# Decay triangles and factors from chunk 1 on, with the gate work moved into the first units, in an mLSTM and mixture-of-experts kernel

## The chip, the cores and the metric

One core of one Trainium2 chip. The metric is the device time in microseconds of one execution; the kernel before took 758.47 us (median of 3 runs, 758.4 to 760.46).

## What is computed

Three layers follow one another on 4 batches of 768 tokens: an mLSTM with 8 heads of 40, a mixture of 8 experts with one expert for each token, and a gated layer of width 2048. Only the first and the beginning of the second are touched. Cut to that:

```python
for t in range(S):                      # S = 768, for each batch and head
    m_new  = maximum(f_gate[t] + m, i_gate[t])
    f_stab = exp(f_gate[t] + m - m_new)
    i_stab = exp(i_gate[t] - m_new)
    m = m_new
    C = f_stab * C + i_stab * outer(v[t], k[t])
    n = f_stab * n + i_stab * k[t]
    y[t] = sigmoid(o_gate[t]) * (C @ q[t]) / maximum(abs(n @ q[t]), 1)
x = y as 3072 tokens of 320
logits = normalised x @ normalised expert_emb.T / tau
expert = argmax(logits)                 # the experts and the last layer come behind it
```

## The kernel before

**Units.** The 768 steps are cut into 6 chunks of 128, and a unit is one chunk of one batch with all 8 heads: 24 units, chunk by chunk, so units 0 to 3 are chunk 0, 4 to 7 chunk 1, and so on. For a unit the kernel forms the scores (k against q, `scores_mm`, L483, 8 products), multiplies them by a 128 x 128 matrix of decays for each head (`scores_w`, L488), multiplies that with the values (`pv`, L546), adds what the state of the chunks before gives (`inter`, L533, `epilogue1`, `epilogue2`), divides and gates (`finish`, L581 and L584, on GpSimd), and brings the state forward (`state`, L497, the three products of weighted keys and values; `state_up`, L514 or L518; `state_decay`, L504).

**Decays, in two ways.** `scan(u)` makes the decay matrices from the row of forget factors of the unit, which `put_dec` stores to memory and `fload` loads back to all 128 partitions. In chunks below `CH`, here 0 and 1, one scan of VectorE runs over 8 x 128 columns (L431). From chunk `CH` on, the scan (L427) makes only the two triangles of 64 x 64 on the diagonal, 8 x 64 columns; the square beside them is a product of two factors, `far_mm` (L439) on TensorE, and ScalarE copies both out (L429, L444).

**Gates and factors.** The gates lie as 96 rows: the 32 pairs of batch and head three times, since the factors are kept as a rounded part and a rest. `gates_m` is the scan of the running maximum (L293), `gates_x` the two sums for the exponent of the forget factor (L298, L299), `gates_xi` that of the input gate, `gates_exp` the exponentials on ScalarE, `gates_z` takes the first column of each chunk out, `gates_e` scans the products of factors from a chunk's (and a half's) beginning (L334). `factors` casts and subtracts for the right factor `fb` (L371, L373), `suffix` makes the products up to a half's end in six steps (L360), for the left factor `fa`; `factor_a` casts that. `spread_b` writes `fb` into 8 masked copies, one for each head (L382, `rhsB`), `spread_a` writes `fa` into 4, one for each batch (L378, `lhsA`): ScalarE. `gates_pe` transposes input weights and decays into token order.

Chunks 0 and 1 have their gates made ahead of the loop; those of chunks 2 to 5 are made together, spread over iterations 0 to 6: the maximum in 0, the sums in 3, exponentials in 3 and 4, the scan of `gates_e` in 4, `gates_pe`, the first half of `suffix` and `spread_b` in 5, the rest in 6.

**Order.** The program is written out by hand (`manual_schedule`): every engine executes its instructions in the order of the text, so the place of a call in the loop over u is its place in each engine's queue. SP issues all the loads and stores, in one queue, with the eight stores that clear the expert slots (`zero_slots`, from iteration `Z0` = 1 on). Iteration u does the scores and the values of neighbouring units, then the routing of unit u-2: `route_t` (L590 to L592, three transpositions of the token rows `x` that GpSimd has finished, copied out by ScalarE, L594), `route_l` (L621 to L623, the logits, copied by VectorE, L625), and once in four units the choice of experts (`route_hot`), the ranks in the expert (`route_rank`, TensorE) and the slots (`route_slot`, VectorE), by which GpSimd scatters the rows.

## Time and profile before

| | us |
|---|---|
| median of 3 runs | 758.47 |
| the profiled execution | 757.6 |
| its span | 755.9 |
| prologue and unit 0, 0 to 17.6: TensorE, VectorE, ScalarE, GpSimd busy | 12.1, 12.0, 7.5, 8.9 |
| chunks 0 and 1, 17.6 to 66.3 | 36.1, 45.2, 23.6, 28.1 |
| chunks 1 to 5, 66.3 to 160.6 | 89.1, 83.3, 50.7, 61.3 |
| last units and first expert, 160.6 to 199 | 32.7, 27.5, 16.7, 22.3 |
| experts and last layer, 199 to 700 | 498.4, 335.4, 247.3, 109.6 |
| end, 700 to 756 | 46.4, 24.3, 21.5, 4.2 |

The engines are PE (TensorE, matmuls; PEld loads their weights), DVE (VectorE), ACT (ScalarE), POOL (GpSimd) and SP (the queue that issues the transfers). Busy time is to be read by stage: TensorE has 95% of the whole span, but in the second row of stages it isn't the busiest. In a timeline the bracket at a line's end gives the time that the engine stood idle ahead of the instruction and what released it.

### The profile page before, as it was taken

The page shows a single profiled execution, that of the slowest core. Times are in us where ns is not written, and L with a number is a line of the kernel's source. Part 1 is how long each engine was busy: PE and PEld are TensorE (multiplying, and loading weights), DVE is VectorE, ACT ScalarE, POOL GpSimd, SP SyncE. Part 2 cuts the span into 40 slices and gives each one's busy share as a digit, 9 for nine tenths or more (in the row PEclk, how much of TensorE's full clock was granted, in tenths as well). Part 3 has the DMA queues.
Part 4 walks back from the last instruction along what each step waited for, and adds up shares of the span by engine and source line. Part 5 has one row for each costly group of instructions (what it writes and reads, how often), then busy time and mean ns, then how long its engine had stood idle before and what let it go on. Part 6 is the DMA issues. An engine that isn't in the chain of part 4 may idle for free.

```text
span 755.9 us, 13328 instructions
## 1 busy us (share of the span) xinstructions
PE 714.8 (95%) x4724; PEld 671.3 (89%) x4724; DVE 527.7 (70%) x1095; ACT 367.3 (49%) x852; POOL 234.3 (31%) x348
## 2 busy tenths in 40 slices
PE   7696999988889999999999999999999999999994
PEld 6696898988889999999998889988889888899994
DVE  7998899896498989899986764545544554445542
ACT  4364455544466666667645443343343343334442
POOL 4562576794243433455401003003003003002011
PEclk9999999999999999999999999999999999999998
DMA  6985887662559767777732121201211201101000
GB/s 190 318 257 178 264 243 235 197 211 84 182 168 241 237 206 192 213 217 255 221 96 67 26 58 46 56 19 42 42 37 36 42 23 36 43 1 46 11 19 19
DMA packets 70490, 95.78 MB, mean 127 GB/s; under 512 B 31794, under 2 KB 56530, under 8 KB 70418
## 3 DMA queue, kind: packets, MB, share of 16 engines
q1 hardware_dynamic: 67346, 86.99, 39.6%
q0 software_dynamic: 3072, 7.89, 2.9%
q8 instruction: 38, 0.62, 0.3%
q14 instruction: 34, 0.28, 0.1%
HBM read 73.73 MB, written 17.19 MB: 120 GB/s over the span
## 4 chain that ended last, share of the span: by engine, by line
issue 41%; PE 24%; POOL 5%; DVE 1%; DMA 1%; POOLq 0%; ACT 0%; SPq 0%; ACTq 0%
PE acc L1230 12%; PE hp L138 11%; POOL out_dram L1275 3%; POOL xr L1381 2%; PE xt L1154 1%; DMA xr<-y 1%; POOL gap L1277 0%; DVE w L121 0%; POOLq L1725 0%; DVE xl L1172 0%; PE xt L1170 0%; DVE hs L1204 0%; DVE xl L1156 0%; DVE w L111 0%; ACT w L118 0%
## 5 line engine op out<-in xcount | busy, mean ns | idle before, releaser
L1230 PE MATMUL acc<-wout,hhl 128*128 128x320 f32 x1152 | 187.0, 309 | 0.0
L1230 PEld LDWEIGHTS acc<-wout,hhl 128*128 128x128 f32 x1152 | 175.9, 188 | 7.4
L1215 DVE TENSOR_TENSOR sg<-hp,sg 128x512 f32<-128x512 f32 (+1 forms) x112 | 68.8, 615 | 93.5 <-ACT sg L1214 87.1
L138 PE MATMUL hp<-xh,win 128*128 128x512 f32 (+1 forms) x560 | 131.0, 364 | 0.0
L1214 ACT ACTIVATE sg<-hp 128x512 f32<-128x512 f32 (+1 forms) x112 | 60.4, 539 | 124.6 <-PE hp L138 124.0
L1275 POOL DMA_INDIRECT out_dram<-o,tokd x24 | 24.0, 1002 | 312.1 <-ACT o L1259 308.5
L1217 DVE TENSOR_TENSOR hhl<-sg,hhl 128x512 fp32r<-128x512 f32 (+1 forms) x112 | 71.4, 637 | 70.3 <-ACT hhl L1216 69.8
L1230 PE MATMUL acc<-w,hs 128*128 128x320 f32 x636 | 104.7, 310 | 2.0 <-ACT hs L1203 1.0
L138 PEld LDWEIGHTS hp<-xh,win 128*128 128x128 f32 x560 | 93.9, 188 | 11.5 <-ACT xh L1420 0.2
L1216 ACT CAST hhl<-sg 128x512 fp32r<-128x512 f32 (+1 forms) x112 | 62.7, 559 | 80.1 <-DVE sg L1215 76.6
L1230 PEld LDWEIGHTS acc<-w,hs 128*128 128x128 f32 x636 | 96.8, 188 | 4.3 <-DVE hs L1204 1.7
L138 PE MATMUL hp<-xl,win 128*128 128x512 f32 (+1 forms) x336 | 85.7, 363 | 0.0
L110 POOL TENSOR_TENSOR w<-r,w 128x256 fp32r<-128x256 f32 x58 | 47.7, 823 | 105.4 <-ACT w L105 87.5
L138 PEld LDWEIGHTS hp<-xl,win 128*128 128x128 f32 x336 | 58.8, 189 | 10.9 <-DVE xl L1421 0.2
L138 PE MATMUL hp<-xh,w 128*128 128x440 f32 (+6 forms) x320 | 66.8, 338 | 0.0
L483 PE MATMUL sp<-qT,kblk 120*128 120x128 f32 x384 | 50.7, 289 | 2.6 <-DVE wm L488 2.6
L138 PEld LDWEIGHTS hp<-xh,w 128*128 128x128 f32 x320 | 51.4, 189 | 1.7
L483 PEld LDWEIGHTS sp<-qT,kblk 120*128 120x128 f32 x384 | 48.2, 204 | 3.4 <-DVE wm L488 2.8
L1203 ACT ACTIVATE hs<-hp 128x440 fp32r<-128x440 f32 (+6 forms) x64 | 30.2, 472 | 40.2 <-PE hp L138 38.0
L546 PE MATMUL op<-vp_in,wm 128*128 128x96 f32 (+1 forms) x368 | 45.3, 277 | 0.1
L546 PEld LDWEIGHTS op<-vp_in,wm 128*128 128x128 f32 x368 | 44.2, 196 | 0.3 <-DVE num L565 0.3
L138 PE MATMUL hp<-xl,w 128*128 128x440 f32 (+6 forms) x192 | 42.8, 331 | 0.0
(324 smaller groups left out, 1123.3 us busy)
## 6 DMA issues: line engine op xcount, KB each, us to landing
...
```

Of the source, the lines that this page charges most:

```text
L110: eng.tensor_tensor(out=t[:, 3 * P:5 * P].rearrange("p (c f) -> p c f", c=2), in0=r1[:, 0:2], in1=hif[:, 0:2], op=ALU.subtract)
L138: nc.tensor.matmul(hp, a, b, start=(i == 0), stop=(i == len(seq) - 1))
L483: nc.tensor.matmul(sp[:, h - hs.start], kblk[u % NLD][0:KR, h // 3, h % 3, :], qT[u][0:KR, h // 3, :], start=True, stop=True)
L546: nc.tensor.matmul(ops[:, h * NW:h * NW + n], wm[u][:, h], vp_in[u % NLD][:, h * DV:h * DV + n], start=True, stop=True)
L1203: nc.scalar.activation(out=hh, in_=hp, func=AF.Relu)
L1214: nc.scalar.activation(out=sg, in_=hp, func=AF.Sigmoid, scale=1.702)
L1215: nc.vector.tensor_tensor(out=g, in0=hp, in1=sg, op=ALU.mult)
L1216: nc.scalar.copy(hh, g)
L1217: nc.vector.tensor_tensor(out=hl, in0=g, in1=hh.bitcast(F32), op=ALU.subtract)
L1230: nc.tensor.matmul(acc_t[blk][i], hl if j == 2 else hh, w[:, DM:2 * DM] if j == 1 else w[:, 0:DM], start=(first and j == 0), stop=(last an ...
L1275: sc = nc.gpsimd.indirect_dma_start(out=out, out_offset=bass.IndirectOffsetOnAxis(ap=tokd[:, ti:ti + 1], axis=0), in_=o[:, i], in_offset=None)
L1381: eng.tensor_tensor(out=xr_t[blk], in0=xr_t[blk], in1=gated[:, t0:t0 + n].unsqueeze(2).to_broadcast([P, n, 3 * P]), op=ALU.mult)
```

## The change

`CH` becomes 1: wide scans of decays are left for units 0 to 3, and units 4 to 23 take triangles and factors. Chunk 0 has its gates made ahead of the loop on 32 rows only, from two loads instead of six; the other four loads (`load_gates(1)`, `load_gates(2)`) stand behind the loads of unit 2. The gates of chunks 1 to 5 are made together, 640 columns instead of 512, in iterations 0 to 3: in 0 `gates_m`, for the two late row groups too, and the masks; in 1 the sums and the exponential of the forget gates; in 2 `gates_z`, the store of the decay rows, the first half of `suffix`, `gates_e` and `spread_b`; in 3 the second half, `gates_pe`, `factor_a`, `spread_a` and the far product of unit 4. Two buffers are shared to make room (`est` is `fd`, `facA` lies in `mm`), and two copies of the masks go from VectorE to GpSimd. `gates_pe0` transposes chunk 0's input weights alone. In the loop `state(u)` stands ahead of `route_t`, `route_rank` behind `pv` and `route_slot` behind `epilogue2`; `scores_w` stands behind the next unit's scan from iteration 4 on; the zeros start in iteration 2.

In the rows below `L` is the line in each kernel's own text (lines of the changed kernel are two or three lower behind the prologue). ScalarE, from the copy of state products ahead of unit 5's rows to the first spread, in iterations 4 and 5 of the kernel before (`fb` the right factor, `rhsB` its spread, `pg` the transposed gates):

```order
L504 ACTIVATE Cst_188<-Cst_188,gdec 120x123 x3
L371 CAST fb<-est 96x256
L552 ACT_TABLE_LOAD
L552 ACTIVATE sg<-kvo 128x320
L395 COPY ei_tok<-pg 128x256
L396 COPY gdec<-pg 120x48
L464 COPY vp_in_122<-ei_tok 128x8
L594 COPY xT<-pr 128x384
L552 ACTIVATE sg<-kvo 128x320
L600 ACTIVATE sq,ss_all<-x 128x320
L504 ACTIVATE Cst_189<-Cst_189,gdec 120x123 x3
L382 ACTIVATE rhsB<-fb,hmask 96x4x64 x8
```

ScalarE in the changed kernel, iterations 2 and 3, from the cast of the right factor to the spreads of the left one:

```order
L364 CAST fb<-fd 96x320
L375 ACTIVATE rhsB<-fb,hmask 96x5x64 x8
L512 ACTIVATE Cst_185<-dC,mask_173 120x3x41 x3
L427 COPY pmb_135<-tri 64x8x64
L565 COPY num<-op 128x328
L393 COPY ei_tok<-pg 128x320
L394 COPY gdec<-pg 120x60
L462 COPY vp_in_119<-ei_tok 128x8
```

and behind these, in iteration 3:

```order
L592 COPY xT<-pr 128x384
L550 ACT_TABLE_LOAD
L550 ACTIVATE sg<-kvo 128x320
L405 COPY enT<-pe__517 128x2x8
L406 COPY enT<-pe__517 64x8
L598 ACTIVATE sq,ss_all<-x 128x320
L357 CAST fa<-mm 96x320
L371 ACTIVATE lhsA<-fa,bmask 96x320 x4
```

Both spreads stand within sixteen rows now, and between them the casts, the gates' copies and a table load. TensorE in iteration 3 of the changed kernel, where `r` is unit 1's logits, `tri` the far product of unit 4 and `sp` its scores; in the kernel before no far product stands ahead of unit 8:

```order
L402 MATMUL pe__517<-ident,emb 128x8
L403 MATMUL pe__517<-ident,emb 128x8
L404 MATMUL pe__517<-ident,emb 128x8
L619 MATMUL r<-enT,xT 128x128
L620 MATMUL r<-enT,xT 128x128
L621 MATMUL r<-enT,xT 128x128
L437 MATMUL tri<-rhsB,lhsA 64x512
L481 MATMUL sp<-qT,kblk_113 128x128 x8
```

The score product of unit 4 stands behind the far product. VectorE in iteration 2, from the denominators `dn` of unit 1, of the kernel before (`pmb` the decays of unit 3 and 4 by wide scans, `fg` the sums of the gates):

```order
L570 SCALAR_TENSOR_TENSOR dn<-num 128x8
L572 TENSOR_SCALAR dn<-dn 128x8
L574 RECIPROCAL dn<-dn 128x8
L431 SCALAR_TENSOR_TENSOR pmb_140<-fb,ident_h 128x1024
L488 TENSOR_TENSOR wm<-sp,pmb_141 128x1024
L570 SCALAR_TENSOR_TENSOR dn<-num 128x8
L572 TENSOR_SCALAR dn<-dn 128x8
L574 RECIPROCAL dn<-dn 128x8
L298 TENSOR_TENSOR fg<-fg,mm 96x512
L299 TENSOR_TENSOR fg<-fg,mm 96x512
L625 COPY logit_all<-r 128x8
L431 SCALAR_TENSOR_TENSOR pmb_141<-fb,ident_h 128x1024
```

VectorE in the changed kernel at the same place (`mm` holds the left factor, `fd` the scanned products, `tri` the triangles of unit 4):

```order
L568 SCALAR_TENSOR_TENSOR dn<-num 128x8
L570 TENSOR_SCALAR dn<-dn 128x8
L572 RECIPROCAL dn<-dn 128x8
L353 TENSOR_TENSOR mm<-mm 96x5x63
L353 TENSOR_TENSOR mm<-mm 96x5x62
L353 TENSOR_TENSOR mm<-mm 96x5x60
L328 SCALAR_TENSOR_TENSOR fd<-fg,fd 96x640
L366 TENSOR_TENSOR fb<-fd,fb 32x320
L367 TENSOR_TENSOR fd<-fd 96x5x64
L334 TENSOR_TENSOR gd<-pairm,fd 32x60
L486 TENSOR_TENSOR wm<-sp,pmb_136 128x1024
L425 SCALAR_TENSOR_TENSOR tri<-fb,id_128 128x512
```

Suffix products, the scan of 640 columns and the work on the factors stand between unit 1's denominators and unit 3's weighting of scores; the scan behind it is the narrow one. TensorE in iteration 7, an ordinary one (`op` the products with values, `pr` the transpositions, `dC` the state products, `ip` the state's part), before:

```order
L546 MATMUL op<-vp_in_124,wm 128x96 x7
L546 MATMUL op<-vp_in_124,wm 128x64
L590 MATMUL pr<-ident,x 128x128
L591 MATMUL pr<-ident,x 128x128
L592 MATMUL pr<-ident,x 128x128
L497 MATMUL dC<-vp_in_122,kw 120x123 x2
L497 MATMUL dC<-vp_in_122,kw 80x82
L533 MATMUL ip<-Cst_189,qT 128x3x41 x2
L533 MATMUL ip<-Cst_189,qT 128x2x41
L439 MATMUL tri<-rhsB,lhsA 64x512
```

and in the changed kernel:

```order
L544 MATMUL op<-vp_in_120,wm 128x96 x7
L544 MATMUL op<-vp_in_120,wm 128x64
L495 MATMUL dC<-vp_in_118,kw 120x123 x2
L495 MATMUL dC<-vp_in_118,kw 80x82
L588 MATMUL pr<-ident,x 128x128
L589 MATMUL pr<-ident,x 128x128
L590 MATMUL pr<-ident,x 128x128
L531 MATMUL ip<-Cst_184,qT 128x3x41 x2
L531 MATMUL ip<-Cst_184,qT 128x2x41
L437 MATMUL tri<-rhsB,lhsA 64x512
```

The state products have moved ahead of the transpositions.

The diff, cut:

```diff
-        R3, HP, CH = 3 * BH, P // 2, 2
+        R3, HP, CH = 3 * BH, P // 2, 1
         ig = ap1.tile([R3, S], F32, name="ig")
         fg = ap1.tile([R3, S], F32, name="fg")
-        for t, g in ((fg, f_gate), (ig, i_gate)):
-            for a in range(3):
+
+        def load_gates(a):
+            for t, g in ((fg, f_gate), (ig, i_gate)):
                 nc.sync.dma_start(out=t[a * BH:(a + 1) * BH], in_=g.rearrange("b h s -> (b h) s"))
+
+        load_gates(0)
...
-        est = ap1.tile([R3, NCH, P], F32, name="est")
+        est = fd
+        facA = mm[:, 0:(NCH - CH) * HP].rearrange("k (c t) -> k c t", t=HP)
...
-        def gates_m(c0, c1):
-            lo, hi = c0 * P, c1 * P
-            nc.vector.tensor_tensor_scan(out=mm[:, 1 + lo:1 + hi], data0=fg[:, lo:hi], data1=ig[:, lo:hi],
-                                         initial=(-1e30 if c0 == 0 else mm[:, lo:lo + 1]), op0=ALU.add, op1=ALU.max)
+        def rows_of(c0, c1, r=None):
+            r = r or slice(0, R3 if c0 else BH)
+            return (lambda t, o=0: t[r, c0 * P + o:c1 * P + o])
+
+        def gates_m(c0, c1, r=None):
+            v = rows_of(c0, c1, r)
+            nc.vector.tensor_tensor_scan(out=v(mm, 1), data0=v(fg), data1=v(ig),
+                                         initial=(-1e30 if c0 == 0 else mm[:, c0 * P:c0 * P + 1]), op0=ALU.add, op1=ALU.max)
 
         def gates_x(c0, c1):
-            lo, hi = c0 * P, c1 * P
-            nc.vector.tensor_tensor(out=fg[:, lo:hi], in0=fg[:, lo:hi], in1=mm[:, lo:hi], op=ALU.add)
-            nc.vector.tensor_tensor(out=fg[:, lo:hi], in0=fg[:, lo:hi], in1=mm[:, 1 + lo:1 + hi], op=ALU.subtract)
-            if c0 < 2:
-                gates_xi(c0, c1)
+            v = rows_of(c0, c1)
+            nc.vector.tensor_tensor(out=v(fg), in0=v(fg), in1=v(mm), op=ALU.add)
+            nc.vector.tensor_tensor(out=v(fg), in0=v(fg), in1=v(mm, 1), op=ALU.subtract)
 
         def gates_xi(c0, c1):
-            lo, hi = c0 * P, c1 * P
-            (nc.gpsimd if c0 else nc.vector).tensor_tensor(out=ig[:, lo:hi], in0=ig[:, lo:hi], in1=mm[:, 1 + lo:1 + hi], op=ALU.subtract)
-
-        def gates_exp_f(c0, c1):
-            lo, hi = c0 * P, c1 * P
-            nc.scalar.activation(out=fg[:, lo:hi], in_=fg[:, lo:hi], func=AF.Exp)
-
-        def gates_exp_i(c0, c1):
-            lo, hi = c0 * P, c1 * P
-            nc.scalar.activation(out=ig[:, lo:hi], in_=ig[:, lo:hi], func=AF.Exp)
-
-        def gates_exp(c0, c1):
-            gates_exp_f(c0, c1)
-            gates_exp_i(c0, c1)
+            v = rows_of(c0, c1)
+            (nc.gpsimd if c0 else nc.vector).tensor_tensor(out=v(ig), in0=v(ig), in1=v(mm, 1), op=ALU.subtract)
+
+        def gates_exp(t, c0, c1):
+            v = rows_of(c0, c1)
+            nc.scalar.activation(out=v(t), in_=v(t), func=AF.Exp)
...
-            if c0 >= CH:
+            if c0:
                 at = lambda t: t.rearrange("k c (a t) -> k c a t", t=HP)[:, c0:c1, :, 0:1]
                 nc.vector.tensor_copy(at(fd), at(fz))
                 nc.vector.memset(at(fz), 0.0)
-                return
-            if c0:
-                nc.vector.tensor_copy(fd[:, c0:c1, 0:1], fz[:, c0:c1, 0:1])
-            nc.vector.memset(fz[:, c0:c1, 0:1], 0.0)
-            if c0 == 0:
+            else:
+                nc.vector.memset(fz[0:BH, c0:c1, 0:1], 0.0)
...
-                factors()
-            gd = wk.tile([BH, n, B * G], F32, tag="gd", name="gd")
+            factors()
+            gd = wk.tile([BH, n, B * G], F32, tag="gd", name="gd", bufs=1)
...
-                nc.vector.tensor_copy(id2[a * HP:(a + 1) * HP],
+                nc.gpsimd.tensor_copy(id2[a * HP:(a + 1) * HP],
...
-        NZ, Z0 = E, 1
+        NZ, Z0 = E, 2
...
             load_v(0)
             gates_m(0, 1)
             gates_x(0, 1)
-            gates_exp(0, 1)
+            gates_xi(0, 1)
+            gates_exp(fg, 0, 1)
+            gates_exp(ig, 0, 1)
             gates_z(0, 1)
-            gates_m(1, 2)
-            gates_x(1, 2)
-            gates_exp(1, 2)
-            gates_z(1, 2)
             nc.sync.dma_start(out=emb, in_=expert_emb)
             norm_en1()
             load_k(1)
...
             load_k(2)
             load_q(2)
             load_v(2)
+            for a in range(1, 3):
+                load_gates(a)
             nc.sync.dma_start(out=tau_sb, in_=tau.unsqueeze(0).to_broadcast([E, 1]))
             keep_warm(ps_1.tile([P, 512], F32, tag="r", name="r"), 6)
-            gates_e(0, 2)
             scan0(0)
             scan0(1)
             kweigh(0)
             scores_mm(0)
-            gates_pe(0, 2)
+            gates_pe0()
             scores_w(0)
             vprime(0, nc.vector)
             scores_mm(1)
...
             for u in range(0, NU - 1):
                 if ok(u - 4):
                     finish(u - 2, nc.gpsimd)
+                if u == 2:
+                    gates_z(1, NCH)
+                    put_dec(1)
                 if ok(u + 2):
                     fload(u + 2)
                 if u == 3:
...
                     state(0)
                     scores_w(1)
                     state_up(0)
-                if u in (2, 5):
+                if u in (2, 3):
                     scores_w(u)
                 if u and ok(u + 1):
                     scan(u + 1)
-                if batch:
-                    route_rank(batch)
-                if u not in (0, 1, 2, 5):
+                if u > 3:
                     scores_w(u)
-                if batch:
-                    route_slot(batch)
-                    pend.extend(batch)
                 if u == 2:
                     norm_en2()
-                if u == 4:
-                    gates_z(2, NCH)
                 if 0 <= u - 1 - W0 < WH:
                     split_half_lo(u - 1 - W0)
                 if u == 0:
                     scan(1)
-                    gates_m(2, NCH)
+                    for a in range(1, 3):
+                        gates_m(0, 1, slice(a * BH, (a + 1) * BH))
+                    gates_m(1, NCH)
+                    masks()
                 if ok(u - 1):
                     pv(u - 1)
+                    if batch:
+                        route_rank(batch)
                     epilogue2(u - 1)
-                if u == 5:
-                    gates_pe(2, NCH)
-                if u in (5, 6):
-                    suffix(u == 6)
-                if u == 1:
-                    masks()
+                if batch:
+                    route_slot(batch)
+                    pend.extend(batch)
+                if u in (2, 3):
+                    suffix(u == 3)
+                if u == 3:
+                    gates_pe(1, NCH)
                 if ok(u + 1):
                     vprime(u + 1)
                     if units[u + 1][1] < CH:
                         kweigh(u + 1)
-                if u == 3:
-                    gates_x(2, NCH)
-                if u == 4:
-                    put_dec(1)
-                    gates_exp_i(2, NCH)
+                if u == 1:
+                    gates_x(1, NCH)
+                if u == 2:
+                    gates_exp(ig, 1, NCH)
+                if u:
+                    state(u)
                 rts = {2: [], 3: [0], 4: [1], 5: [2], 6: [3, 4]}.get(u, [u - 2] if ok(u - 2) else [])
                 if rts:
                     route_t(rts[0])
                 if u == NU - 2:
                     inter(u + 1, True)
-                if u > 4:
+                if u > 2:
                     sigm(u)
                 elif u < 2:
                     sigm(u + 1)
...
                     order_consts()
                 if u == 2:
                     finish(0, nc.gpsimd)
-                if u:
-                    state(u)
                 if u == 3:
                     prep_en()
                 if len(rts) > 1:
                     route_t(rts[1])
                     route_l(rts[0])
                 inter(u)
-                if ok(u + 1):
+                if ok(u + 1) and u != 3:
                     far_mm(u + 1)
                 for i in rts[-1:]:
                     route_l(i)
...
                     route_cnt(batch)
                 batch, newb = newb, None
                 state_decay(u)
+                if u == 1:
+                    gates_exp(fg, 1, NCH)
+                    gates_xi(1, NCH)
+                if u == 2:
+                    gates_e(1, NCH)
+                    spread_b(0, H)
                 if u == 3:
-                    sigm(u)
-                    gates_exp_f(2, NCH)
-                    gates_xi(2, NCH)
-                if u == 4:
-                    gates_e(2, NCH)
-                    sigm(u)
+                    factor_a()
+                    spread_a()
+                    far_mm(4)
                 for i in range(0 if u < US else 1 if u < NU - 5 else 2):
                     if pend:
                         scatter(pend.pop(0))
                 if ok(u + 1) and units[u + 1][1] >= CH:
                     far_out(u + 1)
                     kweigh(u + 1)
-                if u == 5:
-                    spread_b(0, H)
-                if u == 6:
-                    factor_a()
-                    spread_a()
                 if ok(u + 3):
                     load_k(u + 3)
                     load_q(u + 3)
```

## Rows read from the trace of the kernel before

**Rows 1.** Stage windows: stretch, its us, each engine's busy us, clock, DMA share, GB/s.

```profile
17.60:66.30 48.70, 36.08 (x283) 34.35 (x283) 45.22 (x70) 23.55 (x70) 28.09 (x39) 0.93 0.89 281
...
66.30:160.60 94.30, 89.11 (x778) 86.06 (x776) 83.33 (x211) 50.70 (x155) 61.31 (x76) 0.98 0.73 223
```

**Rows 2.** Timeline of TensorE: start us, duration, line, output<-inputs, idle time before and its releaser.

```profile
37.84 2.62 PE L483 MATMUL sp<-qT,kblk 120*128 120x128 f32 x16 [2.65 <-DVE wm L488]
...
66.31 3.48 PE L483 MATMUL sp<-qT,kblk 120*128 120x128 f32 x16
...
74.12 1.95 PE L483 MATMUL sp<-qT,kblk 120*128 120x128 f32 x16
```

**Rows 3.** Windows, columns as in rows 1: TensorE's pause and what follows it.

```profile
61.30:65.50 4.20, 0.00 (x0) 0.00 (x0) 3.95 (x9) 1.33 (x6) 2.56 (x4) 1.00 0.71 208
66.30:69.80 3.50, 3.50 (x25) 3.44 (x23) 3.09 (x12) 1.66 (x4) 0.00 (x0) 0.52 0.47 138
```

**Rows 4.** Timeline of the prologue, columns as in rows 2: SP's queue and VectorE.

```profile
2.19 1.35 SPq L158 DMA_DIRECT2D ig<-in_i_gate_dram  x3
...
12.40 0.34 SPq L282 DMA_DIRECT2D fb<-dec  x1
...
5.79 0.42 DVE L293 TENSOR_TENSOR_SCAN mm<-fg,ig 96x128 f32<-96x128 f32 x1 [1.29 <-DMA ig<-in_i_gate_dram]
...
9.96 0.15 DVE L327 COPY fd<-fg 96x1 f32<-96x1 f32 x1 [0.45 <-ACT fg L309]
...
17.55 2.29 DVE L431 TENSOR_TENSOR_SCAN pmb<-fb,ident_h 128x1024 f32<-128x1024 f32 x1 [1.47 <-DMA fb<-dec]
```

**Rows 5.** Timeline of VectorE; last, one group by form: busy us, mean ns.

```profile
25.17 1.31 DVE L350 COPY id<-ident 64x512 f32<-64x512 f32 x2
...
32.64 0.20 DVE L574 RECIPROCAL dn<-dn 128x8 f32<-128x8 f32 x1
...
39.14 0.64 DVE L298 TENSOR_TENSOR fg<-fg,mm 96x512 f32<-96x512 f32 x1
39.81 1.09 DVE L299 TENSOR_TENSOR fg<-fg,mm 96x512 f32<-96x512 f32 x1
...
45.88 1.21 DVE L334 TENSOR_TENSOR_SCAN est<-fg,fd 96x512 f32<-96x512 f32 x1
...
55.69 2.15 DVE L360 TENSOR_TENSOR facA<-facA 96x252 f32<-96x252 f32 x3
...
L360 DVE TENSOR_TENSOR facA<-facA 96x252 f32<-96x252 f32 x1 | 0.4, 364 | 0.0
```

**Rows 6.** Timeline of ScalarE; last, the state copies by form: busy us, mean ns.

```profile
47.54 1.28 ACT L552 ACT_TABLE_LOAD   x1
48.84 0.47 ACT L552 ACTIVATE sg<-kvo 128x320 f32<-128x320 f32 x1
...
52.97 3.29 ACT L382 ACTIVATE rhsB<-fb,hmask 96x256 fp32r<-96x256 f32 x8
...
L514 ACT ACTIVATE Cst<-dC,mask 120x123 f32<-120x123 f32 x12 | 3.5, 363 | 1.8 <-PE dC L497 1.7
```

**Rows 7.** An ordinary iteration: window, waits from 74 to 157 us, timeline.

```profile
128.00:134.60 6.60, 6.16 (x56) 5.99 (x55) 5.17 (x12) 3.63 (x12) 5.24 (x6) 1.00 0.62 186
...
DVE logit_all L625 <- PE r L623: 7.6, 10, 1.4
...
PE pr L590 <- POOL x L584: 4.2, 9, 0.8
...
136.10 1.71 POOL L581 TENSOR_TENSOR sg<-sg,dn 128x320 f32<-128x320 f32 x1
...
137.89 0.81 POOL L584 TENSOR_TENSOR x<-num,sg 128x320 f32<-128x320 f32 x1
...
138.75 0.33 PE L590 MATMUL pr<-ident,x 128*128 128x128 f32 x1 [0.44 <-POOL x L584]
...
139.14 0.73 PE L497 MATMUL dC<-vp_in,kw 128*120 128x123 f32 x6
```

6 lines of the change are left out of this document (4 added, 2 removed).

## The prediction

> **What bounds the kernel now.** I read the stage windows first. From 17.6 to 66.3 us VectorE is busy 45.2 of 48.7 us while TensorE has 36.1 [rows 1]: there the time is made by VectorE's queue, which holds the wide decay scans of units 2 to 7 and the gate work of chunks 2 to 5. From 66.3 to 160.6 us TensorE is busy 89.1 of 94.3 us, and a closed ring of all four engines sets the pace. The second view is the timeline at the score products, the first TensorE work of each unit: unit 4 starts at 37.84, waiting for VectorE; unit 7 at 66.31; unit 8 at 74.12 [rows 2]. The third is the clock: TensorE did nothing from 61.3 to 65.5, and afterwards ran at 0.52 of full speed, its 1.2 GHz level [rows 3], so that unit 7's product took 3.48 us where unit 8's took 1.95 [rows 2]. Everything behind unit 8 is untouched except for an order on TensorE, so the question has two parts: when does unit 8's score product start, and how long is one iteration behind it?
>
> **Prologue: a gain of 2.2 us at unit 1's scan.** Six gate loads stand first in SP's queue; three of them take 1.35 us to issue [rows 4], so the four that are moved back give 1.8 us to every load behind. The store of the decay row no longer waits for chunk 1's gates either, where VectorE waited 0.45 for an exponential [rows 4]; I count 0.4. Unit 1's scan waits for a broadcast issued at 12.40 and starts at 17.55 [rows 4], 5.15 us later. With the issue at 10.2 it starts at 15.3. The VectorE work that is taken out of the prologue (chunk 1's scans and sums) isn't counted again, because that load ends last either way.
>
> **Units 1 to 3 on VectorE: the point E, where the factor scan of all five chunks ends.** I carry the end of unit 1's denominator, 32.64 + 0.20 = 32.84 [rows 5], to the changed order, in which the same instructions stand in front of it and these come and go:
> - 2.25 off for the prologue, 1.3 off for the two mask copies that go to GpSimd [rows 5].
> - The two row groups of the gates loaded late: two scans of 0.42 us [rows 4], 0.84 at least. SP issues the last of these loads at about 15 us; at the 5.15 us of the broadcast in the same queue it lands at 20, where VectorE is through with unit 1's scan at 17.6. That makes up to 2.9; at the 2.2 us in which the first gate loads land (issued by 3.54, used at 5.79 [rows 4]), 0.84. I take 2.2, near the broadcast, since it is the same stretch of the same queue.
> - Five chunks where four stood: 0.3 for the longer maximum scan; the two sums 0.64 and 1.09 [rows 5] become 1.6 to 2.1, I take 1.9; 0.9 for the exponential that VectorE now waits for, with 0.4 of copies and zeroing.
>
> That is 32.84 - 2.25 - 1.3 + 2.2 + 0.3 + 1.9 + 0.9 + 0.4 = 35.0. Then come the first three suffix products, 2.15 us before [rows 5]; one of them took 0.36 where GpSimd left it alone [rows 5], so 1.3 to 2.6 with five chunks, I take 2.2. The factor scan, 1.21 us for 512 columns [rows 5], is 1.5 for 640. E = 38.7 us, between 36.0 and 39.7. Unit 4's scan is half as long, but it lies behind E, beside ScalarE's work.
>
> **From E to unit 4's score product: ScalarE takes over.** On TensorE the far product of unit 4 now stands directly ahead of unit 4's score product, and it needs both spread factors. Behind E on ScalarE, in order: the 8 right spreads, 3.29 us for 256 columns [rows 6], 3.6 for 320; a table load, 1.28 [rows 6]; 4 left spreads at the rate of the 8, 1.85; 18 small ones (three state copies, casts, other copies, a sigmoid, a square, and the two VectorE subtractions between them) and the far product, which I take at 0.34, a little under the 0.36 of a state copy [rows 6], 6.45. Sum 13.2. VectorE's second three suffix products fit beside it. Unit 4 starts at 38.7 + 13.2 = 51.9, between 49.2 and 52.9, where it started at 37.84.
> The table load shows 1.28 us and the sigmoid behind it starts at once, 48.84 after 47.54 [rows 6]. The Trainium skill (ScalarE: Activation LUTs, What ACT_TABLE_LOAD costs) puts a drain of about 1380 ns on top, 2.66 us for each switch of the set. By that the chain would be 1.4 us longer and the time 761.6; the trace doesn't agree, and the row decides.
>
> **Units 4 to 7.** All gate work is done by then, so TensorE sets the pace: 6.16 us busy in an ordinary iteration of 6.60 [rows 7], I take 6.2; iteration 6 has a second transposition, 0.4 us from 138.75 to 139.14 [rows 7], and a logit product that I put at twice that, 1.2 more. TensorE has stood still for some 4 us ahead of unit 4, as it did ahead of unit 7, so I charge the same loss of clock, 3.48 - 1.95 = 1.5. Unit 8 starts at 51.9 + 1.5 + 3 x 6.2 + 7.4 = 79.4, against 74.12: **a loss of 5.3 us**, between 1.1 (E at 36.0, and the clock stays up) and 6.3. Put shortly: four wide scans become narrow, worth 1 us each on VectorE, but the whole making of the factors now stands in front of unit 4, where three more units covered it.
>
> **State products ahead of transposes.** From unit 8 on TensorE waits at the transposes for the token rows of GpSimd in 9 iterations, 4.2 us in all, 0.8 at most [rows 7]. The three state products have their operands by then and take 0.73 us with the overlap [rows 7], some 0.6 of TensorE's time, so they fill all of these waits but what goes over 0.6: 3.9 us. They also used to stand between the transposes and the logit product, for which VectorE waits 7.6 us in 10 iterations [rows 7]. What decides is whether the rows then come earlier: in the ring shown, GpSimd's gating product is stretched to 1.71 us while VectorE's scan runs, and the transposes start at 138.75 after 0.44 of waiting [rows 7]. With logits 0.6 us earlier the scan starts and ends earlier, so the stretched product ends earlier too. I take a gain of 3.6; nothing is the lower end, 4.6 (TensorE's own pace in all iterations) the upper.
>
> **The rest, at nothing.** The rank products behind the probability products wait no longer for the one-hot rows, but units 20 to 22 are held by VectorE there. Slots made later delay the last four scatters by a microsecond or two, an estimate from the probability products that now stand ahead of them; the loads behind are waited for by nothing in the ring. Zeros a unit later: eight stores move by one unit each and leave unit 4's loads alone; the last lands about when the first scatter wants it.
>
> **Sum.** +5.3 - 3.6 = +1.7 us on the profiled execution, 757.6 us with a span of 755.9: 759.3. The median of the runs, 758.47, is 0.9 above that execution; the forecast is 760.2.
>
> **Rivals.**
> *Slower: the ring keeps its length.* From one transposition to the next run ScalarE's copy, sigmoid, square and decay, the far copy, then GpSimd's three products, one of them stretched to 1.71 by VectorE's scan. If this ring is 6.6 us long by itself, TensorE only waits somewhere else and the reorder gives at most 0.5: 758.47 + 5.3 - 0.5 = 763.3, and 764.3 with E at its late end. For it: GpSimd goes from the stretched product to the next without a gap. Against it: the next took 0.81 [rows 7]; without the stretch the ring is 6.6 - 0.9 = 5.7, below TensorE's 6.2. It decides from a gain under 2.5 us. The Trainium skill (GPSIMD Engine Reference, Key points) says that GpSimd and VectorE contend when VectorE has two SBUF inputs; by that rule the stretch stays wherever the scan falls, which is this rival.
> *Faster: the gate work packs well.* The late gate rows land before VectorE comes to them, GpSimd leaves the sums and suffix products alone (E at 36.0), unit 4 starts at 49.2: a loss of 2.6, or 1.1 if the clock stays up. With the reorder at 4.6 this is 758.47 - 2.0 to - 3.5: 755.0 to 756.5. For it: one suffix product at 0.36. Against it: 2.15 - 0.36 leaves 0.9 for each of the other two.
> *It doesn't do what it says:* the narrow scans save nothing as units 4 to 7 are TensorE's, and the state products gain nothing because the rows follow: loss of 1.1 to 2.6 alone, 759.6 to 761.1.
>
> **How the numbers follow.** A measurement of this kernel can tell 0.3% from no change, 756.2 to 760.7. Forecast, 0.44, spread 758.5 to 762.5: 0.26 within, 0.18 slower. Ring keeps its length, 0.20: slower. Packs well, 0.24: 0.20 faster, 0.04 within. Doesn't do it, 0.06: 0.04 within, 0.02 slower. Left over, 0.06: 0.04 faster, 0.02 within. Sum: faster 0.24, within 0.36, slower 0.40. The range leaves a tenth on each side: from the packed case's 755.0 to the ring's late end, 764.3.
>
> **What would show it.** In the changed trace: unit 1's scan near 15.3; VectorE waiting up to 2.5 us for gate rows behind it; the 640-column factor scan ending near 38.7; ScalarE without a gap behind that; TensorE idle, then unit 4's score product near 52 at the lower clock; unit 8's near 79; no wait for the token rows at the transposes, and iterations of 6.2 to 6.3. It is wrong if unit 4 starts before 48 (packing), or if the iterations stay at 6.6 (ring).

## The result

| kernel | median us | ratio to before, 95% interval |
|---|---|---|
| before | 758.43 (758.33 to 760.46, 4 runs) | |
| changed | 769.89 (766.37 to 771.2, 4 runs) | 1.0137 [1.0098, 1.0176] |

The changed kernel is slower by 1.4%. Forecast were 760.2 us and a range up to 764.3; the time lies outside it. Its profiled execution took 770.71 us with a span of 769.0, 13.1 more than before.

First the places at which the prediction measured: the score products in the timeline of TensorE (start, duration), of unit 23 in the kernel before, then of units 4, 5, 8 and 23 in the changed one.

```profile
174.78 1.95 PE L483 MATMUL sp<-qT,kblk 120*128 120x128 f32 x16
...
56.09 3.62 PE L481 MATMUL sp<-qT,kblk 120*128 120x128 f32 x16
...
64.30 1.95 PE L481 MATMUL sp<-qT,kblk 120*128 120x128 f32 x16
...
85.69 1.95 PE L481 MATMUL sp<-qT,kblk 120*128 120x128 f32 x16
...
188.22 3.01 PE L481 MATMUL sp<-qT,kblk 120*128 120x128 f32 x16
```

Unit 4 starts at 56.09 where the prediction had 51.9 and the kernel before 37.84; unit 8 at 85.69 where it had 79.4, against 74.12 [rows 2]; unit 23 at 188.22, against 174.78 before. So 11.6 of the 13.1 us are lost ahead of unit 8, 1.9 more up to unit 23, and 0.3 come back at the end.

Next the windows of the changed kernel (columns as in rows 1): the stage in which VectorE set the time, TensorE's pauses ahead of unit 4, and unit 4's first products.

```profile
17.60:66.30 48.70, 29.05 (x180) 27.61 (x180) 30.58 (x53) 21.12 (x55) 13.67 (x28) 0.72 0.56 157
...
43.90:56.00 12.10, 6.10 (x30) 5.24 (x31) 6.15 (x12) 9.63 (x27) 0.72 (x1) 0.50 0.53 168
56.10:59.70 3.60, 3.60 (x19) 3.60 (x17) 0.13 (x1) 2.62 (x7) 2.02 (x3) 0.50 0.07 20
```

VectorE, busy 45.2 us of this stage before [rows 1], has 30.6 now. The work is less, as the change meant it, but what lies in it takes longer, because the engines wait for one another. TensorE has 6.1 of 12.1 us ahead of unit 4 and runs at 0.50 of full speed, 1.2 GHz, there and in unit 4's products.

Why the factors come late, in the timeline of VectorE (idle time ahead of an instruction and its releaser in the bracket): unit 1's scan, the maximum scans of the two late row groups, that of all chunks, the two sums, unit 1's denominators, the suffix products and the factor scan.

```profile
16.39 2.29 DVE L429 TENSOR_TENSOR_SCAN pmb<-fb,ident_h 128x1024 f32<-128x1024 f32 x1 [3.46 <-DMA fb<-dec]
21.36 0.41 DVE L300 TENSOR_TENSOR_SCAN mm<-fg,ig 32x128 f32<-32x128 f32 x1 [2.67 <-DMA ig<-in_i_gate_dram]
22.12 0.42 DVE L300 TENSOR_TENSOR_SCAN mm<-fg,ig 32x128 f32<-32x128 f32 x1 [0.34 <-DMA ig<-in_i_gate_dram]
22.57 1.55 DVE L300 TENSOR_TENSOR_SCAN mm<-fg,mm,ig 96x640 f32<-96x640 f32 x1
...
28.30 1.13 DVE L305 TENSOR_TENSOR fg<-fg,mm 96x640 f32<-96x640 f32 x1
29.47 1.82 DVE L306 TENSOR_TENSOR fg<-fg,mm 96x640 f32<-96x640 f32 x1
...
38.44 0.20 DVE L572 RECIPROCAL dn<-dn 128x8 f32<-128x8 f32 x1
38.56 2.34 DVE L353 TENSOR_TENSOR mm<-mm 96x315 f32<-96x315 f32 x3
40.82 1.48 DVE L328 TENSOR_TENSOR_SCAN fd<-fg,fd 96x640 f32<-96x640 f32 x1
```

The point E of the prediction, the end of the factor scan, is 40.82 + 1.48 = 42.3, not 38.7. VectorE waits 2.67 and 0.34 us for the late gate rows.

And from there to unit 4: on ScalarE the copy of transposed rows, the table load and the sigmoid, the cast of the left factor and the left spreads; on VectorE the logit copy, behind which the left factor's rest stands; on TensorE the far product.

```profile
50.05 0.48 ACT L592 COPY xT<-pr 128x384 f32<-128x384 f32 x1 [0.89 <-PE pr L590]
50.55 1.28 ACT L550 ACT_TABLE_LOAD   x1
51.84 0.47 ACT L550 ACTIVATE sg<-kvo 128x320 f32<-128x320 f32 x1
...
53.04 0.44 ACT L357 CAST fa<-mm 96x320 fp32r<-96x320 f32 x1
55.00 1.92 ACT L371 ACTIVATE lhsA<-fa,bmask 96x320 fp32r<-96x320 f32 x4 [1.52 <-DVE fa L359]
...
54.28 0.17 DVE L623 COPY logit_all<-r 128x8 f32<-128x8 f32 x1 [3.45 <-PE r L621]
...
55.61 0.69 PE L437 MATMUL tri<-rhsB,lhsA 96*64 96x512 f32 x1 [1.37 <-ACT lhsA L371]
```

From E to unit 4 it is 13.8 us, against 13.2 forecast.

### The profile page after: what moved, and what is told of

It is laid out like the page before. It is cut to its first block, busy times and chain, and to the rows that moved or that the text cites. A ratio compares the mean times of both kernels' runs of the same rounds, so it can differ in the third digit from the quotient of the medians.

```text
span 769.0 us, 13342 instructions
## 1 busy us (share of the span) xinstructions
PE 720.2 (94%) x4725; PEld 675.9 (88%) x4725; DVE 521.4 (68%) x1088; ACT 371.0 (48%) x857; POOL 232.0 (30%) x349
## 3 DMA queue, kind: packets, MB, share of 16 engines
q1 hardware_dynamic: 67442, 85.94, 39.1%
## 4 chain that ended last, share of the span: by engine, by line
issue 41%; PE 23%; POOL 5%; DVE 2%; DMA 1%; POOLq 0%; ACT 0%; SPq 0%; ACTq 0%
PE acc L1226 11%; PE hp L138 10%; POOL out_dram L1271 3%; POOL xr L1377 2%; PE xt L1150 1%; DMA xr<-y 1%; DVE w L121 0%; POOL gap L1273 0%; DVE hs L1200 0%; DVE xl L1152 0%; DVE w L111 0%; DVE fr L1295 0%; POOLq L1721 0%; DVE xl L1168 0%; PE xt L1166 0%
## 5 line engine op out<-in xcount | busy, mean ns | idle before, releaser
L138 PEld LDWEIGHTS hp<-xh,win 128*128 128x128 f32 x560 | 94.0, 188 | 11.4 <-ACT xh L1416 0.2
L481 PEld LDWEIGHTS sp<-qT,kblk 120*128 120x128 f32 x384 | 50.4, 211 | 1.5 <-DVE pmb L454 0.9
L544 PE MATMUL op<-vp_in,wm 128*128 128x96 f32 (+1 forms) x368 | 44.3, 274 | 1.4 <-DVE wm L486 1.4
```

Of the source, the lines that this page charges most:

```text
L138: nc.tensor.matmul(hp, a, b, start=(i == 0), stop=(i == len(seq) - 1))
L481: nc.tensor.matmul(sp[:, h - hs.start], kblk[u % NLD][0:KR, h // 3, h % 3, :], qT[u][0:KR, h // 3, :], start=True, stop=True)
L544: nc.tensor.matmul(ops[:, h * NW:h * NW + n], wm[u][:, h], vp_in[u % NLD][:, h * DV:h * DV + n], start=True, stop=True)
```

## Experiments: which part of the change costs what

In what follows an iteration is counted from the score product of its unit to that of the next. The theory after the two traces (A): triangles and early factors lose 11.6 us ahead of unit 8; state products ahead of the transpositions win 1.9 us in the eleven ordinary iterations behind it (8, 9, 11 to 13, 15 to 17, 19 to 21: 69.0 us against 70.9); and ranks behind the probability products, slots behind the denominators lose 3.7 us in the four with a choice of experts (10, 14, 18, 22: 33.5 against 29.8). The last was an edit that the prediction had put "at nothing". In the changed kernel, iteration 14, VectorE reads the ranks at 132.75 and TensorE waits to write logits into the same bank (both are the tile `r`):

```profile
132.75 0.14 DVE L687 TENSOR_TENSOR sl__1490<-r,oh_all 128x32 f32<-128x32 f32 x1
...
133.03 0.46 PE L619 MATMUL r<-enT,xT 128*128 128x128 f32 x2 [1.65 <-DVE sl__1490 L687]
```

Four kernels put these parts together one by one. `e1_state_alone` is the kernel before with

```diff
+                if u:
+                    state(u)
                 rts = {2: [], 3: [0], 4: [1], 5: [2], 6: [3, 4]}.get(u, [u - 2] if ok(u - 2) else [])
...
-                if u:
-                    state(u)
```

> The kernel before with one move: the state products ahead of the transpositions. Theory A (from the two traces: the eleven ordinary iterations behind unit 8 are shorter by 1.9 us in sum): 756.5 us, between 755.5 and 757.5, and the wait at the transpositions for the token rows, 4.2 us before, near 1. Rival (the ring keeps its length): 758.4, with the waits moved to another instruction.

`e2_order_alone` is that with ranks and slots moved too:

```diff
-                if batch:
-                    route_rank(batch)
...
-                if batch:
-                    route_slot(batch)
-                    pend.extend(batch)
...
                     pv(u - 1)
+                    if batch:
+                        route_rank(batch)
                     epilogue2(u - 1)
+                if batch:
+                    route_slot(batch)
+                    pend.extend(batch)
```

> The kernel before with the change's whole order of the ordinary loop: state products ahead, rank products behind the probability products, slots behind the denominators. Theory A (the slots are made later, and the logit product waits for the bank that they read; 3.7 us in the four iterations 10, 14, 18, 22): 756.5 + 3.7 = 760.2, between 758.8 and 761.2. Rival (those four iterations are longer for another reason, such as late loads): as the kernel with the state products alone, 756.5.

`e3_ranks_back` is the changed kernel with that second diff reversed, `e4_triangles_alone` with both reversed.

> The changed kernel with rank products and slots where they stood before. Theory A: 769.9 - 3.7 = 766.2, between 764.5 and 767.5, with no wait of the logit product for the slots. Rival (another reason): 769.9.

> The changed kernel with the order of the ordinary loop undone altogether (state products behind the transpositions, ranks and slots as before): triangles, factors and early gates alone. Theory A: the loss stands in front of unit 8, 11.6 us by the trace, so 766.2 + 1.9 = 768.1, between 766.5 and 770. Rival (part of the loss behind unit 8 belongs to the order): under 765.

| kernel | median us | ratio to before, 95% interval |
|---|---|---|
| e1, state products | 757.29 | 0.9987 [0.9971, 1.0003] |
| e2, with ranks and slots | 758.44 | 0.9996 [0.9980, 1.0012] |
| e3, changed, ranks and slots back | 768.47 | 1.0122 [1.0089, 1.0154] |
| e4, triangles and early gates alone | 768.36 | 1.0127 [1.0097, 1.0157] |

The median of before was 758.63 here. The triangles with the early gates make nearly all of the loss: 9.7 us in e4, somewhat less than theory A had. In the kernel before the state products win about 1 us and the ranks and slots lose about 1; in the changed one the state products win nothing that shows (768.47 with them, 768.36 without) and the ranks and slots lose 1.4. Each of these is within the intervals. For its other parts theory A doesn't hold as it stood: e2 and e3 lie outside their ranges, and e1, inside its own, has 70.8 us in the eleven ordinary iterations, where the kernel before has 70.9, and still waits 2.9 us at the transpositions.

Nor are the 11.6 us ahead of unit 8 all the triangles'. In e4 unit 8 starts at 82.87, 8.8 us behind the kernel before and 2.8 ahead of the changed one. Of these 2.8 us 1.0 is ahead of unit 4: in iteration 3 of the changed kernel the transpositions stand behind state products that themselves wait for ScalarE, so that ScalarE's copy of the transposed rows waits 0.89 us (at 50.05, above); in e4 it doesn't wait, and from E to unit 4 it is 12.8 us instead of 13.8. Another 0.6 is iteration 6 (7.84 us against 7.23), and 1.0 iteration 7, by the ranks (7.55 against 6.56, and 6.55 in e3). In e4, on ScalarE and TensorE:

```profile
48.98 0.47 ACT L592 COPY xT<-pr 128x384 f32<-128x384 f32 x1
...
82.87 1.95 PE L481 MATMUL sp<-qT,kblk 120*128 120x128 f32 x16
```

The traces show the ranks more plainly than the time: from unit 8 to unit 23 it takes 102.5 us in the changed kernel and 98.9 with ranks and slots back, 98.5 in e1 and 102.1 in e2, 3.6 us both times. In iterations 10, 14, 18 and 22 alone it is more, 33.5 against 27.0 and 27.6 against 32.1, but the ordinary iterations move the other way by 2.9 and 0.8. With ranks and slots back, slots are read at 131.13 and the logits follow without a wait:

```profile
131.13 0.17 DVE L687 TENSOR_TENSOR sl__1475<-r,oh_all 128x32 f32<-128x32 f32 x1
...
132.00 0.38 PE L619 MATMUL r<-enT,xT 128*128 128x128 f32 x2
```

The bank is only part of it. In iteration 22, which has 1.9 of the 3.7 us of theory A, TensorE doesn't wait for it. The kernel before stands twice there, 1.52 us ahead of the last rank products and the products with the values, and 0.57 ahead of the state's part (`ip`); with the ranks behind those products it stands once, for 2.08, and afterwards ran at 0.50 of full speed instead of 1.00. From the state's part to unit 23's scores it then takes 4.36 us instead of 2.31. Timelines and windows of the kernel before and of the changed one:

```profile
169.49 0.22 PE L671 MATMUL r<-oh_all,ones 128*128 128x24 bf16 x3 [1.52 <-DVE oh_all L651]
...
172.47 1.57 PE L533 MATMUL ip<-Cst,qT 120*128 120x123 f32 x12 [0.57 <-ACT xT L594]
...
172.47:174.70 2.23, 2.23 (x19) 2.19 (x20) 1.30 (x5) 1.17 (x4) 1.79 (x3) 1.00 0.20 78
...
183.86 2.86 PE L531 MATMUL ip<-Cst,qT 120*128 120x123 f32 x12 [2.08 <-ACT xT L592]
...
183.86:188.20 4.34, 4.34 (x19) 4.25 (x20) 1.50 (x7) 1.73 (x5) 2.10 (x4) 0.50 0.10 38
```

That the medians show 1.2 us (e1 to e2) or 1.4 (changed to e3) of the 3.6 has two reasons in sight. A profile is one execution: e1's was the shortest of its ten (754.89, up to 759.31), e2's the second longest (759.8, from 756.86); what the others lose, and where, isn't shown. And e3 gives 2.5 us back behind unit 23: from its scores to the first expert's accumulation it takes 23.9 us, the changed kernel 21.3, as VectorE's last weighting of scores stands for 2 us there and TensorE behind it. What releases it, the profile doesn't settle.

## Experiments: why the factors come late

Theory B: VectorE's queue up to the factor scan, then ScalarE's up to the left spreads, decide when unit 4 starts; each microsecond taken out of either comes off. Each kernel here adds one edit to the one before it. `e5_gates_sooner`, the changed kernel with

```diff
             fload(1)
+            for a in range(1, 3):
+                load_gates(a)
             load_k(2)
             load_q(2)
             load_v(2)
-            for a in range(1, 3):
-                load_gates(a)
```

> The changed kernel with the four late gate loads issued ahead of unit 2's loads instead of behind them. Theory B (the gate work on VectorE is late because it waits for these rows, 2.67 and 0.34 us behind unit 1's scan): the waits go, the 640-column factor scan ends near 39.3 instead of 42.3, unit 4's score product starts near 53.1 instead of 56.1, 766.9 us (765.5 to 768.5). Rival (another wait stands behind it, such as unit 2's loads, now later): unit 4 within 0.5 of 56.1, 769.9.

`e6_input_gate_sooner`:

```diff
+                if u == 1:
+                    gates_xi(1, NCH)
                 if ok(u + 1):
                     vprime(u + 1)
...
                 if u == 1:
                     gates_exp(fg, 1, NCH)
-                    gates_xi(1, NCH)
```

> As the kernel with the gate loads sooner, and GpSimd's subtraction for the input gates issued ahead of the values of unit 2, so that it no longer runs beside VectorE's two sums. Theory B (the sums took 1.13 and 1.82 us because GpSimd worked beside them; 0.8 and 1.36 is what 640 columns cost at the rate of before): factor scan and unit 4 earlier by another 0.8 us, 766.1. Rival (it stretches the scan or the product that it now stands beside as much): no change.

`e7_sigmoid_later`:

```diff
-                if u > 2:
+                if u > 3:
                     sigm(u)
...
                     far_out(u + 1)
                     kweigh(u + 1)
+                if u == 3:
+                    sigm(u)
```

> As the kernel before it in this list, and unit 3's sigmoid with its table load moved behind the spreads. Theory B (ScalarE's queue leads from the factor scan to unit 4): unit 4's score product earlier by another 1.7 us, near 50.6, 764.4. Rival (VectorE or TensorE leads there): under 0.4 us.

`e8_kept_warm`, with `wt_` in the bank of `ip`:

```diff
+                if u == 3:
+                    keep_warm(wt_, 10)
                 if u:
                     state(u)
...
                     prep_en()
+                    keep_warm(wt_, 10)
...
+                    keep_warm(wt_, 8)
                     far_mm(4)
```

> As the kernel before it in this list, and 28 idle products on TensorE (identity by identity, into a bank that nobody reads) in the three pauses ahead of unit 4's score product. Theory B (the pauses cost the clock): unit 4's score product 1.95 us instead of 3.6 and the logit products ahead of it 0.7 shorter, 762.3. Rival (the clock falls all the same, or the idle products stand in the way): 764.4 or more.

| kernel | median us (before 758.58 beside e5 to e8) | factor scan ends | unit 4 starts | unit 8 starts |
|---|---|---|---|---|
| changed | 769.89 | 42.3 | 56.09 | 85.69 |
| e5, gate rows sooner | 767.26 | 40.9 | 54.65 | 83.52 |
| e6, input gates sooner | 767.40 | 38.9 | 52.70 | 81.46 |
| e7, sigmoid later | 764.36 | 39.1 | 51.18 | 80.85 |
| e8, idle products | 766.43 | 41.2 | 55.03 | 83.04 |

VectorE's timeline in e5 (unit 1's scan and the late scans) and e6 (unit 1's scan and the second sum):

```profile
17.45 2.29 DVE L429 TENSOR_TENSOR_SCAN pmb<-fb,ident_h 128x1024 f32<-128x1024 f32 x1 [4.53 <-DMA fb<-dec]
...
19.77 1.23 DVE L300 TENSOR_TENSOR_SCAN mm<-fg,ig 32x128 f32<-32x128 f32 x2
21.04 1.55 DVE L300 TENSOR_TENSOR_SCAN mm<-fg,mm,ig 96x640 f32<-96x640 f32 x1
...
16.13 2.29 DVE L429 TENSOR_TENSOR_SCAN pmb<-fb,ident_h 128x1024 f32<-128x1024 f32 x1 [3.65 <-DMA fb<-dec]
...
27.07 0.82 DVE L306 TENSOR_TENSOR fg<-fg,mm 96x640 f32<-96x640 f32 x1
```

In e5 the late scans start behind unit 1's scan without a wait, so the 3.0 us are gone; but in this execution that scan itself starts at 17.45 instead of 16.39, held by its own load, and about half is given back: 1.4 us at unit 4, 2.6 in the median. The edit isn't shown to be the reason: e6 and e7 have the same loads in the same order and start it at 16.13 and 16.36, e8 at 17.49. In e6 the second sum falls from 1.82 to 0.82 us once GpSimd doesn't work beside it. The first stays at 1.13. Unit 4 comes 1.95 us sooner than in e5, 1.0 by the sum and the rest by that load, and yet the median doesn't fall: in the profiles loads of decay rows hold later scans longer than in e5 (5.5 against 3.3 us between 66 and 180). In e7 the stretch from factor scan to unit 4 shrinks from 13.8 to 12.1, the 1.7 of the table load and the sigmoid: ScalarE's queue does lead there. The median falls by 3.0, more than this explains.

The clock, in the windows of e7 and e8 around unit 4 (columns as in rows 1), each with unit 4's score product:

```profile
40.70:51.10 10.40, 6.13 (x30) 5.25 (x31) 6.18 (x12) 7.96 (x25) 0.72 (x1) 0.50 0.65 207
51.20:55.00 3.80, 3.80 (x20) 3.80 (x18) 0.20 (x2) 3.75 (x8) 2.23 (x4) 0.50 0.08 20
...
51.18 3.62 PE L481 MATMUL sp<-qT,kblk 120*128 120x128 f32 x16
...
44.30:55.00 10.70, 10.70 (x76) 10.51 (x76) 4.69 (x10) 6.43 (x21) 0.72 (x1) 0.79 0.46 153
55.00:58.80 3.80, 3.71 (x33) 3.54 (x31) 1.38 (x2) 3.75 (x8) 2.19 (x4) 1.00 0.10 30
...
55.03 1.95 PE L481 MATMUL sp<-qT,kblk 120*128 120x128 f32 x16
```

With TensorE busy through the stretch ahead of it, unit 4's product runs at 2.4 GHz: 1.95 us, not 3.62, and unit 5 follows 6.61 behind unit 4 instead of 8.27. So the 1.5 us of the prediction for the clock were about right. The trial as a whole doesn't gain: the products are more than the pauses hold, at the lower clock 10 of them take 4.61, so E to unit 4 is 13.9 again. E itself is 2.1 us later than in e7, by loads of decay rows ahead of the scans of units 1 and 2, and the four executions lie far apart (764.34 to 768.74).

Then all of it together, ranks and slots back, and fewer idle products (`f1_mended`); the embedding work out of VectorE's way (`f3_mended_trimmed`); and idle products in the last unit's pause (`f4_tail_warm`):

```diff
                 if u == 3:
+                    keep_warm(wt_, 8)
                     gates_pe(1, NCH)
+                    keep_warm(wt_, 5)
...
+                    keep_warm(wt_, 3)
                     far_mm(4)
```

> The changed kernel with gate loads and the input gates' subtraction sooner, unit 3's sigmoid behind the spreads, ranks and slots where they stood before, and fewer idle products than in the trial before (8 ahead of the gates' transpositions, 5 behind them, 3 ahead of the far product). Theory B (what was found adds up: 764.4 for the kernel with the sigmoid later, 1.3 off for the ranks, 1.7 off for the clock): 761.4 us, between 760 and 763; unit 4's score product near 51 at 1.95 us. Rival (idle products cost as much as the clock gives, ranks give nothing here): 764.4.

```diff
+            norm_en2()
             batch, newb, pend = None, None, []
...
-                if u == 2:
-                    norm_en2()
```

> As the mended kernel, and the five small operations on the expert embeddings (1.74 us on VectorE between unit 3's scan and the factors) moved into VectorE's pause ahead of unit 1's scan. Theory B (VectorE's queue leads to the factor scan): unit 4 another 1.7 us earlier, 759.7. Rival (loads lead there): no change against the mended one.

```diff
+            keep_warm(dC.rearrange("p g f -> p (g f)"), 6)
             pv(u, True)
```

> As the mended and trimmed kernel, and six idle products on TensorE ahead of the last unit's product with the values, where TensorE stood for 1.8 us and ran at the lower clock afterwards. Theory B (with ranks back the last unit loses what the order won, by the clock): 761.9 - 2.5 = 759.4, the first expert products 21.5 us behind unit 23's scores instead of 23.7. Rival (VectorE or the scatters lead there): 761.9.

They took 764.0 (1.0053 [1.0032, 1.0074]), 761.85 (1.0042 [1.0023, 1.0061]) and 762.21 us (1.0043 [1.0027, 1.0058]). f3 falls by 2.2 us where 1.7 were expected, f1 and f4 don't fall as expected. Of f3's gain the trace shows E 1.75 us sooner than in f1, but unit 4 only 0.8 (50.38 against 51.16). f1's unit 23 starts at 178.53, 9.7 us ahead of the changed kernel's, and the first expert comes 25.3 behind it, 4 more than there: its last product with the values took 3.65 us after a pause. In f4 the pause is filled and the product takes 1.97, by TensorE's timeline of f1 and f4:

```profile
184.37 3.65 PE L544 MATMUL r<-vp_in,wm 128*128 128x96 f32 x16 [1.82 <-DVE wm L486]
...
183.12 1.97 PE L544 MATMUL r<-vp_in,wm 128*128 128x96 f32 x16
```

But f3, without the idle products, had 2.03 in its own profile, and the medians are equal: the rival held. So with what was found mended, the changed kernel still stands 3 us above the one before.

The same trimming on the kernel before, `f2_before_trimmed`: the diff of e1 and of f3, the mask copies on GpSimd and the masks behind `gates_m(2, NCH)`.

> The kernel before with the state products ahead, the two mask copies on GpSimd, both mask sums and the five embedding operations moved forward (beside the maximum scan, and into the pause ahead of unit 1's scan), tau's load ahead of them. Theory B (VectorE's queue makes the time from 17.6 to 66.3 in the kernel before, so the 1.3 and 1.7 us taken out of it come off the end): 757.3 - 1.3 - 1.4 = 754.6, between 753.5 and 756. Rival (a load of a decay row waits there instead): 757.3.

757.53 us, 0.9982 [0.9966, 0.9999], no better than e1 alone: the rival. VectorE reaches unit 4's scan sooner, and waits there for the decay row, 4.03 us where it waited 1.93 in e1:

```profile
35.16 2.30 DVE L431 TENSOR_TENSOR_SCAN pmb<-fb,ident_h 128x1024 f32<-128x1024 f32 x1 [4.03 <-DMA fb<-dec]
```

## Experiments: why the state products win so little

Forecast were 3.6 us, about 1 was measured. In e1 the waits at the transpositions (74 to 157 us) fell only from 4.2 [rows 7] to 2.9; an ordinary iteration, from GpSimd's and VectorE's timelines and TensorE's:

```profile
PE pr L590 <- POOL x L584: 2.9, 8, 0.4
...
129.48 0.72 POOL L581 TENSOR_TENSOR sg<-sg,dn 128x320 f32<-128x320 f32 x1
130.28 1.60 POOL L584 TENSOR_TENSOR x<-num,sg 128x320 f32<-128x320 f32 x1
...
129.69 1.59 DVE L427 TENSOR_TENSOR_SCAN tri<-fb,id 128x512 f32<-128x512 f32 x1 [0.17 <-DMA fb<-dec]
...
131.94 0.33 PE L590 MATMUL pr<-ident,x 128*128 128x128 f32 x1 [0.23 <-POOL x L584]
```

The first gating product starts ahead of the scan now and takes 0.72 us, but the second starts while the scan runs and takes 1.60: the stretch has moved from one product to the next, and the rows are late as before. Between 74 and 157 us twelve gating products are stretched in e1, six first and six second ones, where nine were in the kernel before. The Trainium skill (GPSIMD Engine Reference, Key points) says that GpSimd contends with VectorE when that has two SBUF inputs; the scan here has two, and the trace agrees, with 1.60 beside it and 0.81 elsewhere [rows 7]. Theory C: the gating products come late because on GpSimd they stand behind the weighted keys, which wait for the far copy. From unit 8 on they go ahead:

```diff
-                if ok(u - 4):
+                if ok(u - 4) and u < 8:
                     finish(u - 2, nc.gpsimd)
...
                     far_out(u + 1)
+                    if 8 <= u + 1 < NU - 1:
+                        finish(u - 1, nc.gpsimd)
                     kweigh(u + 1)
```

`g1_gating_first` is e1 with that, `g2_gating_alone` the kernel before with that alone, `g3_mended_gating_first` the kernel f3 with it from unit 5 on.

> The kernel before with the state products ahead, and GpSimd's two gating products ahead of its weighted keys from unit 8 on instead of behind them. Theory C (the ring keeps its length because the gating products stand behind the weighted keys, which wait 1.2 us for the far copy, and so run beside VectorE's scan, where one of them takes 1.6 us): they run before the scan, the rows are ready before TensorE comes to them, iterations of 6.2 to 6.3 us instead of 6.5, 757.3 - 3.5 = 753.8, between 752.5 and 755.5. Rival (VectorE, busy 5.6 to 6.3 us in each of these iterations, or the weighted keys, now later, hold the ring): 757.3 or more.

> The kernel before with the gating products ahead of the weighted keys from unit 8 on, state products behind the transpositions as before. Theory C: the waits at the transpositions, 4.2 us in all, go without the state products being moved, 754.5, between 753 and 756. Rival: 758.5 or more.

> The mended and trimmed kernel with triangles from chunk 1 on, and the gating products ahead of the weighted keys from unit 5 on. Theory C: 761.9 - 3.5 = 758.4, between 757 and 760. Rival: 761.9 or more.

| kernel | median us (before 759.19 in this round) | ratio, 95% interval |
|---|---|---|
| g1, state products and gating first | 755.83 | 0.9952 [0.9937, 0.9967] |
| g2, gating first alone | 756.51 | 0.9960 [0.9947, 0.9973] |
| g3, mended, gating first | 759.93 | 1.0008 [0.9996, 1.0021] |

Theory C holds, at about three quarters of its size in all three by the ratios; g1 and g2 lie 0.3 and 0.5 us above their ranges, g3 just inside. The timelines of GpSimd, VectorE and TensorE in g1:

```profile
128.26 0.72 POOL L581 TENSOR_TENSOR sg<-sg,dn 128x320 f32<-128x320 f32 x1 [1.24 <-DVE dn L574]
129.06 0.81 POOL L584 TENSOR_TENSOR x<-num,sg 128x320 f32<-128x320 f32 x1
129.82 1.65 POOL L470 TENSOR_TENSOR kw<-kvo,pmb 128x320 f32<-128x320 f32 x1
...
129.29 1.66 DVE L427 TENSOR_TENSOR_SCAN tri<-fb,id 128x512 f32<-128x512 f32 x1
...
131.52 0.83 PE L497 MATMUL dC<-vp_in,kw 128*120 128x123 f32 x6 [0.68 <-POOL kw L470]
```

Both gating products start ahead of the scan and take 0.72 and 0.81 us, and no transposition waits. The stretch has moved once more, here to the weighted keys, 1.65, and the state products wait for those, 0.68 us in this iteration, 1.0 in all between 74 and 157. There it falls on the keys twice, and six times on the weighted values (`vp_in`, L463), for which no engine waits. g1 is the fastest kernel here, 0.5% under the one before, and g2 shows that the gain is the gating's; the state products add 0.7 us to it, within the spread. g3 against g1 is the triangles from chunk 1 on, mended as far as this study went, against the kernel before with the same order: 4.1 us slower.

## The prediction, point by point

Forecast were 1.7 us more in the span, measured 13.1. Of the 11.4 between them 6.3 stand ahead of unit 8 (E 3.6, E to unit 4 0.6, units 4 to 7 2.1) and 5.1 behind it, where a gain of 3.6 was forecast and 1.5 were lost.

- **Prologue, right in kind, half its size.** Unit 1's scan starts at 16.39 where 15.3 was forecast: the broadcast was issued at 10.83 and took 5.56.
- **E, the first term that failed:** 42.3 against 38.7, outside its own bounds. 1.1 us of it is unit 1's scan. 1.7 is the late gate rows: from the end of that scan to the maximum scan of all chunks it took 3.9 us, where 2.2 had been taken and 2.9 was the upper bound; the last of these loads was issued at 16.74 to 17.16, not at about 15, and from there to its use it took 5.0 us, near the broadcast's 5.15 by which it was priced. 1.1 is the two sums, 3.0 us against 1.9, with 2.1 as the upper bound: the second had GpSimd's new subtraction beside it (e6). The rest came 0.3 shorter; suffix products (2.34 against 2.2) and factor scan (1.48 against 1.5) were right. Two terms came out past their upper ends and the prologue, which had none, late as well; the prediction had a rival in which the gate work packs well and none in which it packs badly.
- **E to unit 4, right in part by luck:** 13.8 against 13.2, with ScalarE leading, as e7 showed. The left spreads were priced at 1.85, but the far product of unit 4 follows the first of the four, 0.6 us behind their start (55.00 to 55.61). Against that stand two waits not seen: 0.89 at the copy of the transposed rows, by the change's own move of the state products, which the prediction counted from unit 8 on only; and 1.52 at the left spreads, as on VectorE the left factor's rest stands behind a logit copy that waits 3.45 us for TensorE. The table load took 1.28 us and the sigmoid followed at once, so the longer price that the prediction turned down was rightly turned down.
- **Units 4 to 7, too low:** 29.6 us against 27.5. The clock cost 3.62 - 1.95 = 1.7, near the 1.5 forecast. Iteration 7, priced as an ordinary one, took 7.55 against 6.2: it has a choice of experts, and its logit product waits 1.15 us as in iteration 14, though the profile names ScalarE as the releaser there; with ranks and slots back (e3) it takes 6.55.
- **State products, the second term that failed:** 3.6 us forecast; about 1 measured in the kernel before, nothing that shows in the changed one. The step that failed is "the stretched product ends earlier too": the stretch passed to the next product, and twelve gating products were stretched instead of nine (e1). The rival that the ring keeps its length was nearly right, by the mechanism that it named.
- **"The rest, at nothing" failed for ranks and slots:** in the traces they cost 3.6 us from unit 8 to unit 23 and 1.0 in iteration 7, partly by a wait for a bank that the prediction didn't look for, partly by a pause in iteration 22 that takes the clock down. In the medians about 1 us of it arrives.

The mended kernel still stands 3 us above the one before; which waits make these 3 us is open.
